# Moving a four-byte tile of GpSimd's from ahead of the SiLU halves to the end of the SBUF allocation

## The chip, the cores and the metric

The kernel runs on one core of a Trainium2 chip. The metric is the device time of one execution in microseconds (us). Three executions of the kernel before took 629.55, 629.67 and 630.14 us, so its median is 629.67 us. A fourth execution was recorded by the profiler; its own time and its span are in the table below.

## What is computed

The input x has 2048 rows of 640 values. The reference, cut to what matters:

```python
xn = layernorm(x)                       # over the 640 columns, no scale, no bias
q, k, v = split(xn @ wqkv)              # 32 heads of 20; wqkv is 640 x 1920
# row i attends to rows i, i-2, ... i-14 (8 rows, 2 apart); rows before 0 masked
s = attention(q, k, v) @ wo             # softmax over the 8; wo is 640 x 640
h = silu(xn @ w1) @ w2                  # w1 is 640 x 1536, w2 is 1536 x 640
out = x + s * silu(h)
```

All arrays are float32.

## The kernel before, in words

**Precision by halves.** TensorE multiplies in the type `float32r`. To keep float32 accuracy every operand of a large product is kept as a high half, rounded to that type, and a low half, the remainder. One product a*b is three matmuls: high by high, low by high, high by low. The halves of the normalized x are `TH` and `TL`, those of the attention's output are `OH` and `OL`, those of silu(xn @ w1) are `SH` and `SL` ("silu's halves"), and those of a weight lie one behind the other in one tile of the ring `w`, which has 7 slots.

**Groups.** The 2048 rows are worked in four groups of 512. A group has 4 row tiles of 128 (the index t). Each group goes through these stages on TensorE, in this order:

- `qkv_phase` (lines 950 to 952, and line 883 for the first quarter of the first group): xn @ wqkv in four quarters of the heads. `TH`/`TL` are stationary (loaded by LDWEIGHTS, 128 x 128), the weights stream past them (the moving operand).
- `ffn_phase`, which weaves `up` (lines 1114 to 1116: one 128-column block of w1 is stationary, `TH`/`TL` stream in rows of 512) with `down` (function `down`, matmuls at lines 990 and 992: `SH` or `SL` is stationary, a block of w2 streams). There are 12 blocks, so 12 `up` and 12 `down` in each group.
- `wo_phase` of the group before stands behind the first `up` (lines 990 and 992 again: `OH`/`OL` stationary, wo streams). For the last group `wo_last` does this at the very end, in another order: row tile by row tile, with the five weight tiles taken one after the other inside.

The products by w2 and by wo have 640 output columns, more than one PSUM bank holds. The helper `tm_mm` (lines 986 to 992) splits each into a matmul of 384 columns (line 990) and one of 256 columns (line 992) with the same stationary operand. The text calls two such matmuls a **pair**. `down` makes 12 pairs for a block: for each of the 4 row tiles `SH` by the high half and `SH` by the low half of w2 (8 pairs), and then for each row tile `SL` by the high half (4 pairs). `wo_phase` makes 3 pairs for each row tile and each of 5 weight tiles.

Between the matmuls the other engines work: ScalarE evacuates PSUM and makes the high halves (line 1127 writes `sh`, line 1128 writes the unrounded copy `sf`), VectorE makes the low halves (line 1129 writes `sl` from `sf` and `sh`) and does the whole attention (lines 768 to 808, tiles `kv`, `q`, `pr`, `l`, `o`). The order of the instructions on all engines comes from a planner (class `Weave`), which works from fixed costs and does not know addresses.

**The tile that moves.** `MARK` is one float32 per partition. At lines 910 to 912 GpSimd runs three subtractions of one column into it. Its value is never read. The instruction exists to make GpSimd wait for a tile of x to be normalized before it goes on.

**Where the tiles lie.** All SBUF tiles come from one pool with one buffer each (line 297, allocations at lines 318 to 349), and lie in a partition in the order of allocation. In the built program each starts at a multiple of 32 bytes. The last of the 7 weight tiles ends at byte 94976 of a partition, a multiple of 256. `epst` (4 bytes), `sd` (32 bytes) and `mark` (4 bytes) follow and take 32 bytes each, so `sh0` starts at 95072. Then come `sh1`, `sh2`, `sl0` to `sl2` (2048 bytes each), `mv`, `z`, `kv`, `q`, `o`, `pr`, `l`, `xin`, `gate`, `xr`, `sf` and `turn`. `th`, `tl` and `w` lie ahead and start at multiples of 256. `OH` and `OL` are views into the same memory as `TH` and `TL`, but 16 floats (64 bytes) further on for `OH` (the constant `OAT`), which is stationary in `wo_phase`.

The text names the place of a tile by what is left when its start is divided by 128: `w`, `TH` and `TL` 0, `OH` and `OL` 64, `sh` and `sl` 96, and `kv`, `q`, `o`, `pr`, `xin`, `gate`, `xr`, `sf`, `turn` 0.

Of the kernel before, what the change touches and what calls it, by code (L numbers as in the profile page):

```python
# [23 lines left out]
T = 4  # L24
# [269 lines left out]
def local_attention_silu_ffn(ctx: ExitStack, tc: tile.TileContext, x, wqkv, wo, w1, w2, out):  # L294
# [20 lines left out]
    def tiles(name, n, shape, dtype=F32):  # L315
        return [sb.tile(shape, dtype, name=f"{name}{i}") for i in range(n)]

    ident = sb.tile([P, P], F32, name="ident")
    def small(name, *shape):
        return sb.tile([P, *shape], F32, name=name)  # L320
# [10 lines left out]
    OH, OL = chunks(TH, OAT), chunks(TL, OAT)  # L331
    TH, TL = chunks(TH, 0), chunks(TL, 0)
    WR = tiles("w", RING, [P, 2 * D], F32R)
    epst, SD, MARK = small("epst", 1), small("sd", 2, T), small("mark", 1)
    SH = tiles("sh", NS, [P, TOK], F32R)
    SL = tiles("sl", NS, [P, TOK], F32R)
    MV = small("mv", T, 2)
# [9 lines left out]
    XR = tiles("xr", 3, [P, D])  # L347
    SF = sb.tile([P, TOK], F32, name="sf")
    TURN = sb.tile([P, TOK], F32, name="turn")
    ACC = [psum.tile([P, TOK], F32, name=f"acc{i}") for i in range(6)]  # L350
    ROT = [psum.tile([P, TOK], F32, name=f"rot{i}") for i in range(2)]
    carry = [dram.tile([2, NQ, 2, T, CQ], F32, name=f"carry{par}") for par in range(2)]
# [5 lines left out]
    def take(kind, n):  # L358
        i = count[kind] % n
        count[kind] += 1  # L360
        return i

    def bank():
        i = take("acc", 6)
        return ACC[i], ("acc", i)

# [20 lines left out]
    def pe(dur, fn, reads, writes, spans=()):  # L387
        add("PE", dur, fn, reads, writes, spans=spans)
        clock[0] += dur
# [262 lines left out]
    def both(k):  # L652
        return [k + (0,), k + (1,)]

    def piece(tile_of, k):
        return tile_of.rearrange("p t d -> p (t d)")[:, k * TOK:(k + 1) * TOK]
# [14 lines left out]
    def join(frm, into, kinto, reads, i, c, hi, lo, at=0.0, of=None):  # L671

        b, kb = frm
        kh, kl = t_keys(i, [c], kinds=["th"]), t_keys(i, [c], kinds=["tl"])
        act(2 * TOK, lambda: nc.scalar.activation(
            into.bitcast(U16).rearrange("p t (n h) -> p h t n", h=2),
            b.bitcast(U16).rearrange("p (h t n) -> p h t n", h=2, t=T), AF.Copy),
            both(kb) + reads, kinto, 150, more=0.3, at=at, spans=chunk_span(of, c, True) if of else ())
        act(TOK, lambda: nc.scalar.activation(hi.rearrange("p (t n) -> p t n", t=T), into, AF.Copy), kinto + reads, kh, 0)
        dve(TOK, lambda: nc.vector.tensor_tensor(  # L680
            out=lo.rearrange("p (t n) -> p t n", t=T), in0=into,
            in1=hi.bitcast(F32).rearrange("p (t n) -> p t n", t=T), op=OP.subtract),
            kinto + reads + kh, kl, 0, lock=True, late=SUB_LATE, spans=chunk_span(of, c) if of else ())

    def turn_x(c, i, at):
        keys = [("xin", t) for t in range(T)]
        by = (TURN, ("turn",)) if c % 2 == 0 else (piece(G, X_BY[c]), ("buf", X_BY[c]))
        to = piece(G, c), ("buf", c)
# [3 lines left out]
    def spare(s, q):  # L692

        return KV[q][:, s, HALO:, :].rearrange("p t m -> p (t m)")[:, :TOK], (("own", "val")[s], q, "x")
# [11 lines left out]
    def turn_o(g, c, i, out, into, at=0.0):  # L706
# [3 lines left out]
        xp = [(piece(XIN, k), ("xp", k)) for k in range(DC)]  # L710
        by, to = ((xp[0], xp[1]), (xp[2], xp[3]), (xp[4], (TURN, ("turn",))), (xp[1], xp[3]))[c]
        if g < NG - 1:
            by, to = (TURN, ("turn",)), (SF, ("sf",))
        if out:
# [118 lines left out]
    def first_quarter(i):  # L833
# [3 lines left out]
        def warm(n, where):  # L837
            for k in range(n):
                nc.tensor.transpose(where[:, tsl(k % T)], ident, ident)
# [64 lines left out]
        for n, step in enumerate(FIRST.split()):  # L904
            if n == len(PARTS):
                pe(0.11 * WARM2, lambda: warm(WARM2, ACC[5]), [], [("acc", 5)])
            (turn if len(step) == 2 else product)(*map(int, step))
# [10 lines left out]
    def qkv_phase(g, i, io):  # L918
        if g == TURNS:
            for c in O_FIRST:  # L920
                by, to = (((TURN, ("turn",)), spare(1, 0)), (spare(0, 1), spare(1, 1)))[c]
                join(to, by[0].rearrange("p (t n) -> p t n", t=T), both(by[1]), [], io, c, OH[io][:, c, :], OL[io][:, c, :])
# [232 lines left out]
    def ffn_phase(g, i, ix, io):  # L1155
# [10 lines left out]
        if g < TURNS:  # L1166
            lent = ((TURN, ("turn",)), spare(1, 0)), (spare(0, 1), spare(0, 0)), ((TURN, ("turn",)), spare(0, 0)), (spare(0, 1), spare(1, 1))
            for v in ((0, 0), (0, 1), (1, 0), (1, 1)):
# [75 lines left out]
```

## Time and profile before

| what | number |
|---|---|
| median of 3 executions | 629.67 us |
| profiled execution, its own time | 629.49 us |
| its span, first to last instruction | 627.7 us |
| TensorE (PE) busy | 621.7 us, 99% of the span |
| weight loads (PEld) busy | 563.1 us |
| VectorE (DVE) busy | 542.7 us |
| ScalarE (ACT) busy | 264.2 us |
| GpSimd (POOL) busy | 114.8 us |
| matmuls | 3415 |

PE is the matmul side of TensorE and PEld its weight loads, which run beside the matmuls. Matmuls are pipelined: the duration of one as the profile shows it is longer than the distance to the next one's start. So where a rate is wanted, the text takes the distance between starts. The difference between the profiled execution's own time and its span, 1.8 us, lies around the program's instructions.

### The profile page before, as it was taken

To read this page: it belongs to the slowest core of one execution; us is meant where nothing else is said; L and a number is where in the kernel's file an instruction comes from. 1 tells how busy PE (TensorE), PEld (TensorE's weight loads), DVE (VectorE), ACT (ScalarE), POOL (GpSimd) and SP (SyncE) were. 2 spreads that over 40 slices of the span, in tenths; PEclk is the share of its full clock that TensorE was granted. 3 is DMA by queue.
4 is the path that set the end of the run, shared out by engine and by line. 5 is a ranking of instruction groups with operands and counts; after the bars stand their busy time and mean duration, and the time that the engine had idled before them with its cause. 6 is when DMAs were issued, how large, how long until landed. Compare 5 with 4: busy or idle time off the path is not lost.

```text
span 627.7 us, 9038 instructions
## 1 busy us (share of the span) xinstructions
PE 621.7 (99%) x3415; PEld 563.1 (90%) x3415; DVE 542.7 (86%) x545; ACT 264.2 (42%) x490; POOL 114.8 (18%) x165
## 2 busy tenths in 40 slices
PE   8999999999999999999999999999999999999997
PEld 7888999998889999999888999999988999999897
DVE  6699899999788988999969999998745999998834
ACT  4445455463536216353434503445543343243220
POOL 5800000001110142111221114211222211111100
PEclk9999999999999999999999999999999999999999
DMA  9999999599999999775899999997599998678652
GB/s 312 292 319 317 317 394 373 187 325 268 257 331 299 310 264 294 236 205 147 203 307 252 317 368 256 331 233 215 141 239 271 294 344 238 202 218 243 192 185 85
DMA packets 99260, 166.07 MB, mean 265 GB/s; under 512 B 31008, under 2 KB 60672, under 8 KB 99216
## 3 DMA queue, kind: packets, MB, share of 16 engines
q1 hardware_dynamic: 72720, 85.77, 48.6%
q0 software_dynamic: 25952, 79.31, 44.1%
q8 instruction: 27, 0.44, 0.3%
q10 hardware_dynamic: 544, 0.41, 0.2%
q14 instruction: 17, 0.14, 0.1%
HBM read 107.91 MB, written 34.16 MB: 226 GB/s over the span
## 4 chain that ended last, share of the span: by engine, by line
PE 98%; DMA 0%; DVE 0%; issue 0%
PE acc L990 23%; PE acc L992 15%; PE acc L950 10%; PE acc L952 10%; PE acc L951 10%; PE rot L1114 9%; PE rot L1116 9%; PE rot L1115 9%; PE acc L883 2%; PE rot L630 1%; DMA xin<-in_A_x_dram 0%; PE rot L867 0%; PE rot L1100 0%; DVE st L852 0%; PE rot L826 0%; DVE gate L1068 0%
## 5 line engine op out<-in xcount | busy, mean ns | idle before, releaser
L990 PE MATMUL acc<-w,sh 128*128 128x384 f32 x384 | 115.2, 338 | 0.0
L950 PE MATMUL acc<-w,th 128*128 128x512 f32 (+2 forms) x300 | 113.2, 377 | 0.0
L952 PE MATMUL acc<-w,th 128*128 128x512 f32 (+2 forms) x300 | 112.8, 376 | 0.0
L951 PE MATMUL acc<-w,tl 128*128 128x512 f32 (+2 forms) x300 | 112.8, 376 | 0.0
L992 PE MATMUL acc<-w,sh 128*128 128x256 f32 x384 | 107.5, 280 | 0.0
L768 DVE TENSOR_TENSOR pr<-q,kv 128x2560 f32<-128x2560 f32 x32 | 90.2, 2819 | 13.3 <-DMA kv<-kv 13.1
L1127 ACT ACTIVATE sh<-rot 128x512 fp32r<-128x512 f32 x48 | 28.7, 599 | 166.0 <-PE rot L1116 165.9
L1114 PE MATMUL rot<-th,w 128*128 128x512 f32 x240 | 94.4, 393 | 0.0
L1116 PE MATMUL rot<-th,w 128*128 128x512 f32 x240 | 93.6, 390 | 0.0
L1115 PE MATMUL rot<-tl,w 128*128 128x512 f32 x240 | 93.5, 390 | 0.0
L800 DVE TENSOR_TENSOR pr<-q,kv 128x2560 f32<-128x2560 f32 x32 | 90.3, 2822 | 0.7
L771 DVE TENSOR_REDUCE l<-pr 128x128 f32<-128x2560 f32 x32 | 90.0, 2814 | 0.3
L558 POOL DMA_DIRECT2D w<-half_q x52 | 37.4, 719 | 236.6 <-DVE pr L805 97.7
L558 POOL DMA_DIRECT2D w<-half_w x72 | 38.6, 536 | 215.1 <-PE acc L992 99.8
L805 DVE TENSOR_TENSOR pr<-pr 128x1280 f32<-128x1280 f32 x64 | 75.5, 1180 | 1.4
L992 PEld LDWEIGHTS acc<-w,sh 128*128 128x128 f32 x384 | 72.5, 189 | 1.1
L990 PEld LDWEIGHTS acc<-w,sh 128*128 128x128 f32 x384 | 72.1, 188 | 1.0
L952 PEld LDWEIGHTS acc<-w,th 128*128 128x128 f32 x300 | 56.3, 188 | 8.8
L951 PEld LDWEIGHTS acc<-w,tl 128*128 128x128 f32 x300 | 56.3, 188 | 8.6
L950 PEld LDWEIGHTS acc<-w,th 128*128 128x128 f32 x300 | 56.3, 188 | 8.5
L990 PE MATMUL acc<-w,sl 128*128 128x384 f32 x192 | 59.0, 338 | 0.0
L727 ACT ACTIVATE kv<-acc 128x320 f32<-128x320 f32 x64 | 28.1, 441 | 69.2 <-PE acc L952 67.9
(115 smaller groups left out, 1040.8 us busy)
## 6 DMA issues: line engine op xcount, KB each, us to landing
w<-half_w POOLq DMA_DIRECT2D x72, 640.0 KB, 5.3
w<-half_q POOLq DMA_DIRECT2D x39, 512.0 KB, 4.9
half_w<-w SPq DMA_DIRECT2D x24, 640.0 KB
kv<-kv SPq DMA_DIRECT2D x16, 560.0 KB
kv<-kv SPq DMA_DIRECT2D x16, 420.0 KB
w<-half_wo POOLq DMA_DIRECT2D x10, 640.0 KB, 5.6
gate<-in_B_w_dram SPq DMA_DIRECT2D x16, 320.0 KB
w<-half_q POOLq DMA_DIRECT2D x13, 384.0 KB, 7.9
```

The lines of the kernel that those rows point to most:

```text
L558: add("POOL", 1.0, lambda: nc.gpsimd.dma_start(both, src), [("half", u), ("half", u, "more")], [kh, kl], due + 10, nbytes=2 * n * P * 4)
L768: dve(2560, lambda t=t: nc.vector.tensor_tensor(out=PR, in0=win(qq[:, t:t + 2, :], W, 0), in1=win(kv[:, 0, t:t + 2, :], W, CQ), op=OP.mult ...
L771: dve(2560, lambda t=t: nc.vector.tensor_reduce(out=l[:, t:t + 2].rearrange("p t w h -> p (t w h)"), in_=PR.rearrange("p t w (h d) -> p (t ...
L800: dve(2560, lambda t=t, v=v: nc.vector.tensor_tensor(out=PR.rearrange("p t w (h d) -> p t (w h) d", d=DH), in0=e[:, t:t + 2].rearrange("p ...
L950: nc.tensor.matmul(o, hi, wh, start=c == 0, stop=False)
L951: nc.tensor.matmul(o, lo, wh, start=False, stop=False)
L952: nc.tensor.matmul(o, hi, wl, start=False, stop=c == DC - 1)
L990: nc.tensor.matmul(a[t][0][:, :CA], st, w[:, :CA], start=first, stop=last)
L992: nc.tensor.matmul(b[t // 2][0][:, h * CB:(h + 1) * CB], st, w[:, CA:], start=first and h == 0, stop=last, skip_group_check=True)
L1114: nc.tensor.matmul(h, wh[:, cs], TH[i][:, c, :], start=c == 0, stop=False)
L1115: nc.tensor.matmul(h, wh[:, cs], TL[i][:, c, :], start=False, stop=False)
L1116: nc.tensor.matmul(h, wl[:, cs], TH[i][:, c, :], start=False, stop=c == DC - 1)
```

## The change

`MARK` is taken out of the line that allocates it between `sd` and `sh0`, and allocated behind `turn`, the last tile of the pool. No instruction, wait, size or order is edited. What follows from the 32-byte starts: `sh0` begins at 95040 instead of 95072, and every tile from `sh0` to `turn` begins 32 bytes lower, so that `sh` and `sl` go from place 96 to place 64, and `kv`, `q`, `o`, `pr`, `xin`, `gate`, `xr`, `sf` and `turn` from place 0 to place 96. `ident`, `th`, `tl`, `w`, `epst` and `sd` stay.

```diff
     WR = tiles("w", RING, [P, 2 * D], F32R)
-    epst, SD, MARK = small("epst", 1), small("sd", 2, T), small("mark", 1)
+    epst, SD = small("epst", 1), small("sd", 2, T)
     SH = tiles("sh", NS, [P, TOK], F32R)
     SL = tiles("sl", NS, [P, TOK], F32R)
     MV = small("mv", T, 2)
...
     SF = sb.tile([P, TOK], F32, name="sf")
     TURN = sb.tile([P, TOK], F32, name="turn")
+    MARK = small("mark", 1)
     ACC = [psum.tile([P, TOK], F32, name=f"acc{i}") for i in range(6)]
```

## The prediction

> **What bounds the kernel now.** I read the page first, for the engines' shares and the chain that ended last.
>
> ```profile
> span 627.7 us, 9038 instructions
> ...
> PE 621.7 (99%) x3415; PEld 563.1 (90%) x3415; DVE 542.7 (86%) x545; ACT 264.2 (42%) x490; POOL 114.8 (18%) x165
> ...
> PE 98%; DMA 0%; DVE 0%; issue 0%
> PE acc L990 23%; PE acc L992 15%; PE acc L950 10%; PE acc L952 10%; PE acc L951 10%; PE rot L1114 9%; PE rot L1116 9%; PE rot L1115 9%; PE acc L883 2%; PE rot L630 1%; DMA xin<-in_A_x_dram 0%; PE rot L867 0%; PE rot L1100 0%; DVE st L852 0%; PE rot L826 0%; DVE gate L1068 0%
> ```
>
> The matmuls fill the span, and 98% of the chain is matmul behind matmul. Lines 990 and 992, which share the pair matmuls of `down` and of the wo stages, hold 38% of it. Next, the view of waits for PE:
>
> ```profile
> PE rot L839 <- POOL ident masks.py:199: 1.4, 1, 1.4
> PE rot L867 <- DVE xin L857: 0.7, 1, 0.7
> ```
>
> These two waits, both in the first microseconds, are all that it lists. So the time is a count of matmuls times the distance from one start to the next, and an edit that adds or removes no instruction can act only through that distance, or by making another engine so late that PE waits. The groups that keep forms apart give the count of the matmuls whose stationary operand moves:
>
> ```profile
> L990 PE MATMUL acc<-w,sh 128*128 128x384 f32 x384 | 115.2, 338 | 0.0
> L992 PE MATMUL acc<-w,sh 128*128 128x256 f32 x384 | 107.5, 280 | 0.0
> ...
> L990 PE MATMUL acc<-w,sl 128*128 128x384 f32 x192 | 59.0, 338 | 0.0
> L992 PE MATMUL acc<-w,sl 128*128 128x256 f32 x192 | 53.8, 280 | 0.0
> ```
>
> That is 384 + 192 = 576 pairs. Then I asked whether a pair costs the same everywhere, in the timeline of PE. One block of `down` (start in us, modelled duration):
>
> ```profile
> 88.87 0.34 PE L990 MATMUL acc<-w,sh 128*128 128x384 f32 x1
> 89.04 0.28 PE L992 MATMUL acc<-w,sh 128*128 128x256 f32 x1
> ...
> 92.39 0.38 PE L630 MATMUL rot<-ident,xin 128*128 128x128 f32 x2
> ```
>
> Between the first and the last row lie 12 pairs (8 by `sh`, 4 by `sl`): 3.52 / 12 = **293.3 ns a pair**. A stretch of `wo_phase`:
>
> ```profile
> 203.53 0.33 PE L990 MATMUL acc<-w,th 128*128 128x384 f32 x1
> 203.70 0.28 PE L992 MATMUL acc<-w,th 128*128 128x256 f32 x1
> ...
> 206.97 0.33 PE L990 MATMUL acc<-w,th 128*128 128x384 f32 x1
> ```
>
> Again 12 pairs of 384 and 256 columns, by the same weight ring: 3.44 / 12 = **286.7 ns**. And `wo_last`:
>
> ```profile
> 608.23 0.34 PE L990 MATMUL acc<-w,th 128*128 128x384 f32 x1
> 608.41 0.28 PE L992 MATMUL acc<-w,th 128*128 128x256 f32 x1
> ...
> 611.83 0.34 PE L990 MATMUL acc<-w,th 128*128 128x384 f32 x1
> ```
>
> 12 pairs: 3.60 / 12 = **300.0 ns**. The reader is to see that the same two instructions run at three paces, with no wait in any of the three stretches. In `down` the stationary operand stands at place 96, in both wo stages at place 64 (`OH`, `OL`), and the streamed weights at place 0 in all three.
>
> **The change part by part.** It adds, removes and reorders no instruction, DMA or wait, so nothing is queued behind anything new. Three things can cost or gain.
>
> *GpSimd's own instruction.*
>
> ```profile
> L910 POOL TENSOR_TENSOR mark<-xin 128x1 f32<-128x1 f32 x3 | 0.6, 195 | 4.0 <-issue 1.8 <-DVE xin L857 1.5 <-POOL w L571 0.7
> ```
>
> Three of 195 ns, which write one column per partition somewhere else. No one reads it: 0.
>
> *The 576 pairs of `down`.* Their stationary operand goes from 96 to 64, which is the very place, against the same ring, that `wo_phase` has. If the place makes the difference, a pair goes from 293.3 to 286.7 ns: 576 x 6.6 = 3.8 us. The bounds are the other rows: no change at all, 0, and the pace of `wo_last`, 576 x (300.0 - 293.3) = 3.9 us more. I take the row nearest to it in form. `down` and `wo_phase` both run the row tiles inside, keep one weight tile for all of them, and use a stationary operand for two or four pairs' matmuls in a row; `wo_last` takes another weight tile and another stationary operand with every pair. From the 3.8 us I take off 0.2: the first pairs behind a change of stage do not yet run at the settled pace (26 such stretches by the order of `up` and `down`, at up to 7 ns). So **-3.6 us**. The Trainium skill speaks against it: "SBUF — State Buffer", in the table under "A bandwidth-pool intuition that's wrong (but worth ruling out)", gives TensorE a second, independent read port for LDWEIGHTS, so where the weights to be loaded lie should not touch the stream, and by that the sum would be 0. The same page, under "Specifications (TRN2)", speaks of 16-byte cachelines, to which both places are equally well aligned: again 0. The three paces above show that something slows a pair by up to 13 ns; they do not show that it is the place.
>
> *Everything else that moves 32 bytes.* VectorE's and ScalarE's operands go from place 0 to 96. Before, there are instructions that already work at 96, beside the like of them at 0:
>
> ```profile
> L1129 DVE TENSOR_TENSOR sl<-sf,sh x48: 679/685/5333, 68.6 to 600.1; 128x512 fp32r<-128x512 f32 x48
> ```
>
> ```profile
> L680 DVE TENSOR_TENSOR tl<-xin,th 128x512 fp32r<-128x512 f32 x16 | 10.9, 684 | 7.4 <-ACT th L679 7.4
> L1127 ACT ACTIVATE sh<-rot 128x512 fp32r<-128x512 f32 x48 | 28.7, 599 | 166.0 <-PE rot L1116 165.9
> L1128 ACT ACTIVATE sf<-rot 128x512 f32<-128x512 f32 x48 | 28.4, 593 | 4.5 <-DVE sl L1129 4.5
> L634 ACT ACTIVATE th<-rot 128x512 fp32r<-128x512 f32 x13 | 7.6, 598 | 15.3 <-PE rot L630 15.3
> ```
>
> Line 1129 reads and writes at 96 in 685 ns (the median), line 680 reads and writes only at 0 in 684; ScalarE writes `sh` at 96 in 599 and `th` at 0 in 598. So I cost these at 0. DMAs into `xin`, `kv`, `xr` and `gate` at 96 do not occur before; no row prices them. The transposes, too, have their stationary operand moved:
>
> ```profile
> L630 PE MATMUL rot<-ident,o 128*128 128x128 f32 x40 | 5.7, 272 | 0.0
> ```
>
> There are 80 in all (40 here, 12 at line 630 by `xin`, 20 at 867, 8 at 826); at the 6.6 ns that the place may be worth to a whole pair they move the time by 0.5 us at most either way, and I take 0.
>
> *What is late next if PE gains.* The tightest place that I found is in the last group, where PE transposes the last rows of the attention's output:
>
> ```profile
> 594.45 0.49 DVE L808 TENSOR_TENSOR o<-pr 128x320 f32<-128x320 f32 x1
> ```
>
> ```profile
> 596.25 0.44 PE L826 MATMUL rot<-ident,o 128*128 128x128 f32 x2
> ```
>
> VectorE is done at 594.94, PE comes at 596.25: 1.31 us to spare. VectorE's run-up to this begins at 477.43, with the first scores of the group, behind a wait that hangs on PE's own progress (the k and v just made, carried over by a DMA):
>
> ```profile
> 477.43 2.83 DVE L768 TENSOR_TENSOR pr<-q,kv 128x2560 f32<-128x2560 f32 x1 [8.11 <-DMA kv<-kv]
> ```
>
> So the gain of the first three groups (432 pairs) moves both, and only that of some 120 pairs in the last group eats into the reserve: 120 x 6.6 = 0.8 us of 1.31. It holds, without much over.
>
> The sum: 629.49 (the profiled execution's own time, 1.8 us of it around the span of 627.7) - 3.6 = 625.9 us. The median of the runs lies 0.2 above the profiled one, so I say **626.0 us**, 0.6% under 629.67.
>
> **Rivals.**
>
> *A, the forecast:* `down` takes the pace of `wo_phase`. For it: form and place are then alike. Against it: `wo_last` has that place as well, and is the slowest. With 0.5 us for the transposes and the same again for pairs that do not settle at once: 625.2 to 627.2 us.
>
> *B, the place does not matter.* The paces then come from the order of the operands: `wo_phase` goes high, high, low through each row tile, `down` takes all high ones first and then all low ones. For it: inside `down` the pace is the same by `sh` and by `sl` (338 and 280 ns in both groups above), so the pace goes with the stage, and each stage has only one place. 629.5 us, between 629.0 and 630.2. That the edit might not move the tiles at all comes to the same time; the sizes and the 32-byte starts leave it little chance.
>
> *C, the slower side: place 64 is the one at which load and stream disturb each other in lockstep.* The stationary operand's reads and the stream's then meet at a fixed distance of half of 128 bytes, and it depends on the order of the matmuls whether they miss each other (286.7) or collide each time (300.0). In `down` they collide, and a pair takes 300.0 ns: 576 x 6.7 = 3.9 us more, 633.4 us. It decides against the forecast as soon as the mean pair of `down` is above 293.3. For it: `wo_last`, with operands at the same places. Against it: `down` has the order of `wo_phase` in all but the low halves.
>
> *D, the other moved tiles cost something.* VectorE's 86% of work, or the k and v transfers, run slower at 96, by an amount that the 685 against 684 ns does not let me expect. From 477.4 to 594.9 VectorE has 117.5 us; a slowdown of 1.1% uses up the 1.31 us, and at 3% the end comes 3.5 - 1.3 = 2.2 us later: 631.7 us without A, about 629 with it.
>
> **How the numbers follow.** Chances: A 0.60, B 0.16, C 0.15, D 0.09. The predicted time is A's, 626.0 us. The range must leave out no more than 2 in 10: from A's lower end, 625.2, over B up to D's 631.7; I leave out C and a little at the edges. A measurement of this kernel can tell about 0.2%, 1.26 us, from no change: faster means under 628.4, slower over 630.9. A is faster, B the same, C and most of D slower: 0.60, 0.16 and 0.24.
>
> **What would show it right or wrong.** Right: in the timeline of the changed kernel 12 pairs of `down` take 3.44 us instead of 3.52; the groups of line 990 by `sh` and `sl` fall from 338 ns towards 332; `wo_phase`, `wo_last` and the `up` matmuls keep their distances; VectorE's groups keep their means; PE's waits stay the two at the start; the span is near 624.1. B is seen in an unchanged 3.52, C in 3.60, D in a new wait of PE at line 826 or in longer means at lines 768 to 808. What would make the prediction wrong is above all that place 64 is not what makes `wo_phase` quick: I have two stages at that place, and they disagree by 13 ns.

## The result and the profile after

| | before | after |
|---|---|---|
| median | 629.64 us (4 runs) | 626.59 us (4 runs, 626.20 to 626.76) |
| ratio, with its 95% interval | | 0.9949 [0.9932, 0.9966] |
| span of the profiled execution | 627.7 us | 625.0 us |

The change made the kernel 3.05 us faster. The page of the changed kernel:

```profile
span 625.0 us, 9038 instructions
...
PE 619.4 (99%) x3415; PEld 559.8 (90%) x3415; DVE 542.8 (87%) x545; ACT 264.3 (42%) x490; POOL 114.8 (18%) x165
...
PE 98%; DMA 1%; DVE 0%; issue 0%
```

The same instructions, the same DVE and ACT, and PE is still the whole chain. Its waits (engine, line, who was waited for, us in total, times, longest) are still the two at the start. One line was added above them, so line 839 is now 840 and 990 is 991:

```profile
PE rot L840 <- POOL ident masks.py:199: 1.4, 1, 1.4
PE rot L868 <- DVE xin L858: 0.4, 1, 0.4
```

The groups whose stationary operand moved:

```profile
L991 PE MATMUL acc<-w,sh 128*128 128x384 f32 x384 | 113.2, 334 | 0.0
L993 PE MATMUL acc<-w,sh 128*128 128x256 f32 x384 | 107.1, 279 | 0.0
...
L991 PE MATMUL acc<-w,sl 128*128 128x384 f32 x192 | 57.8, 332 | 0.0
L993 PE MATMUL acc<-w,sl 128*128 128x256 f32 x192 | 53.6, 279 | 0.0
```

Before, these were 338 and 280 ns. Their distances show it better. One block of `down` in the timeline of PE, first row to last 12 pairs:

```profile
229.17 0.33 PE L991 MATMUL acc<-w,sh 128*128 128x384 f32 x1
229.34 0.28 PE L993 MATMUL acc<-w,sh 128*128 128x256 f32 x1
...
232.61 0.40 PE L1115 MATMUL rot<-th,w 128*128 128x512 f32 x1
```

3.44 / 12 = 286.7 ns, exactly the pace of `wo_phase`, where it was 293.3. But `wo_last`, none of whose operands moved, changed as well. Two rows of the same timeline, 12 pairs apart:

```profile
606.09 0.33 PE L991 MATMUL acc<-w,th 128*128 128x384 f32 x1
...
609.53 0.33 PE L991 MATMUL acc<-w,th 128*128 128x384 f32 x1
```

3.44 / 12 = 286.7 ns too; before it was 300.0. And the `up` matmuls, not moved either, became slower at their beginning. A run of 30 of them, from its first row to the first pair behind it, before:

```profile
232.90 0.40 PE L1114 MATMUL rot<-th,w 128*128 128x512 f32 x1
...
239.71 0.34 PE L990 MATMUL acc<-w,sh 128*128 128x384 f32 x1
```

and after:

```profile
232.61 0.40 PE L1115 MATMUL rot<-th,w 128*128 128x512 f32 x1
...
239.45 0.34 PE L991 MATMUL acc<-w,sh 128*128 128x384 f32 x1
```

6.81 us against 6.84; in the trace's nanoseconds 6810 against 6846. Before, the distances begin 235, 227, 226, 227; after, they begin 235, 234, 235, 225, 230, 236, 229, 232, 231 and only then stay at 226 to 227. This occurs in the 17 runs of `up` that follow a `down`, each 36 ns longer. The kernel before had such long runs too, behind `wo_phase`, the stage that ran at 286.7 ns there:

```profile
219.01 0.40 PE L1114 MATMUL rot<-th,w 128*128 128x512 f32 x1
...
225.86 0.34 PE L990 MATMUL acc<-w,sh 128*128 128x384 f32 x1
```

6.85 us for 30 matmuls (6848 ns), and 6849 ns behind the other two passes of `wo_phase`. So a run of `up` starts slower behind pairs at 286.7 ns than behind pairs at 293.3, and after the change `down` is such a stage as well.

One difference lies in the very first microseconds, in the twenty transposes of the identity that keep TensorE busy before data arrive:

```profile
L840 PE MATMUL rot<-ident 128*128 128x128 f32 x20 | 4.5, 424 | 1.4 <-POOL ident masks.py:199 1.4
```

Before it was 374 ns on average, and in e1 and e2 of the experiments below 400 and 417: the first ones come 213 ns apart and later ones 109, and how many come slowly differs from trace to trace (13 of the 19 distances before, all of them after, in e4 and in e5). No tile of theirs moved, so I do not count it as the change's, but no second profile of one kernel shows how much of it is chance.

Summed over all matmuls, from each start to the next, the two traces differ by: `down` -3.36 us, `wo_last` -0.65, `up` +0.62, all of `qkv` +0.21, all transposes +0.48 (0.34 of it the twenty at the start with the wait behind them). The sum is -2.70, the difference of the spans (627.7 and 625.0).

### The profile page after: what moved, and what is told of

The parts are those of the page before. It is cut to its first block, busy times and chain, and to the rows that moved or that the text cites. A ratio compares the mean times of both kernels' runs of the same rounds, so it can differ in the third digit from the quotient of the medians.

```text
span 625.0 us, 9038 instructions
## 1 busy us (share of the span) xinstructions
PE 619.4 (99%) x3415; PEld 559.8 (90%) x3415; DVE 542.8 (87%) x545; ACT 264.3 (42%) x490; POOL 114.8 (18%) x165
## 4 chain that ended last, share of the span: by engine, by line
PE 98%; DMA 1%; DVE 0%; issue 0%
PE acc L991 22%; PE acc L993 15%; PE acc L953 10%; PE acc L951 10%; PE acc L952 10%; PE rot L1117 9%; PE rot L1116 9%; PE rot L1115 9%; PE acc L884 2%; PE rot L631 1%; DMA xin<-in_A_x_dram 1%; PE rot L868 0%; PE rot L1101 0%; DVE st L853 0%; PE rot L827 0%; DVE gate L1069 0%
## 5 line engine op out<-in xcount | busy, mean ns | idle before, releaser
L991 PE MATMUL acc<-w,sh 128*128 128x384 f32 x384 | 113.2, 334 | 0.0
L769 DVE TENSOR_TENSOR pr<-q,kv 128x2560 f32<-128x2560 f32 x32 | 90.2, 2819 | 12.6 <-DMA kv<-kv 8.8
L801 DVE TENSOR_TENSOR pr<-q,kv 128x2560 f32<-128x2560 f32 x32 | 90.3, 2822 | 0.7
```

What stands on the lines that cost most here:

```text
L769: dve(2560, lambda t=t: nc.vector.tensor_tensor(out=PR, in0=win(qq[:, t:t + 2, :], W, 0), in1=win(kv[:, 0, t:t + 2, :], W, CQ), op=OP.mult ...
L801: dve(2560, lambda t=t, v=v: nc.vector.tensor_tensor(out=PR.rearrange("p t w (h d) -> p t (w h) d", d=DH), in0=e[:, t:t + 2].rearrange("p ...
L991: nc.tensor.matmul(a[t][0][:, :CA], st, w[:, :CA], start=first, stop=last)
```

## The experiments

The first theory: the place of the stationary operand of `down` sets the pace of its pairs. Its rivals: the other tiles that moved (kv, q, pr, xin and so on); the order of a stage's matmuls rather than any place (B). `small` in the diffs allocates a tile, and a tile of 4 to 32 bytes takes 32.

**e1: only silu's halves move.**

```diff
-    epst, SD, MARK = small("epst", 1), small("sd", 2, T), small("mark", 1)
+    epst, SD = small("epst", 1), small("sd", 2, T)
     SH = tiles("sh", NS, [P, TOK], F32R)
     SL = tiles("sl", NS, [P, TOK], F32R)
+    MARK = small("mark", 1)
```

> MARK is allocated right behind silu's halves: sh and sl go from place 96 to 64 as in the changed kernel, every tile behind them (mv, kv, q, o, pr, xin, gate, xr, sf, turn) stays where it was before. Theory 1 (the place of the stationary operand sets the pace of a pair): the whole gain, 626.6 us within 0.5, 12 pairs of down in 3.44 us. Rival (the other moved tiles brought it, or a part of it): 629.6 us, or something between. Side question: wo_last ran at 300 ns a pair before and at 287 after, though none of its operands moved; if it inherits the pace from the stage ahead of it, it runs at 287 here.

Measured 626.45 us, ratio 0.9949 [0.9934, 0.9964]: the whole gain. 12 pairs of `down` took 3.45 us, `wo_last` ran at 286.7 ns.

**e2: only the rest moves.**

```diff
     SL = tiles("sl", NS, [P, TOK], F32R)
+    PAD = small("pad", 24)
```

> The kernel before with 96 idle bytes behind silu's halves: sh and sl stay at place 96, all tiles behind them go from place 0 to place 96, as in the changed kernel. Theory 1: no gain, 629.6 us within 0.5, 12 pairs of down in 3.52 us, wo_last at 300 ns. Rival (the rest brings the gain): about 626.6. My rival D of the prediction (VectorE or the transfers are slower at 96): over 630, with longer means at lines 768 to 808.

Measured 629.90 us, 1.0003 [0.9993, 1.0012]: nothing. From first row to last 12 pairs:

```profile
230.20 0.34 PE L991 MATMUL acc<-w,sh 128*128 128x384 f32 x1
...
233.73 0.40 PE L1115 MATMUL rot<-th,w 128*128 128x512 f32 x1
```

3.53 us, and `wo_last` at 300. The trace has one wait of PE that the kernel before does not have, 0.4 us at line 1115 for ScalarE's `sf`, 68 us into the span; the changed kernel, with `sf` at the same place, has none there. VectorE at place 96 is as quick as at 0, in the changed kernel's groups and here:

```profile
L801 DVE TENSOR_TENSOR pr<-q,kv 128x2560 f32<-128x2560 f32 x32 | 90.3, 2823 | 0.7
L769 DVE TENSOR_TENSOR pr<-q,kv 128x2560 f32<-128x2560 f32 x32 | 90.2, 2819 | 13.0 <-DMA kv<-kv 9.0 <-DMA kv<-carry 3.8
L772 DVE TENSOR_REDUCE l<-pr 128x128 f32<-128x2560 f32 x32 | 90.1, 2815 | 0.3
```

The page of before has 2822, 2819 and 2814. So rival D of the prediction falls, and e1 and e2 together show that the gain is that of `sh` and `sl`.

**e3: `sh` at 64, `sl` at 96.**

```diff
     SH = tiles("sh", NS, [P, TOK], F32R)
+    MARK = small("mark", 1)
     SL = tiles("sl", NS, [P, TOK], F32R)
```

(MARK is taken out of its old line here as well.)

> MARK lies between sh and sl: sh at place 64, sl at 96, the rest as before. Theory 1, pair by pair: the 384 pairs by sh take 286.7 ns and the 192 by sl 293.3, so two thirds of the gain, 627.5 us within 0.5. Rival (the pace belongs to the stage as a whole, as a state in which the matmuls have settled): sh and sl keep one common pace, 286.7 or 293.3, and the time is 626.6 or 629.6.

Measured 628.60 us, 0.9982 [0.9973, 0.9991]. Neither expectation holds: not the 627.5 of the theory, and no common pace. Two blocks of `down` in a row, each 8 pairs by `sh` and then 4 by `sl`:

```profile
253.67 0.34 PE L991 MATMUL acc<-w,sh 128*128 128x384 f32 x1
...
255.98 0.34 PE L991 MATMUL acc<-w,sl 128*128 128x384 f32 x1
...
257.15 0.34 PE L991 MATMUL acc<-w,sh 128*128 128x384 f32 x1
...
259.52 0.34 PE L991 MATMUL acc<-w,sl 128*128 128x384 f32 x1
```

The first 8 pairs follow an `up` and take 2.31 us, 289 ns a pair; the second 8 follow pairs by `sl` at 96, and take 2.37, 296 ns. (Before and after the change, the two blocks of such a run differ by less than 2 ns a pair.) Pair by pair (384 + 256 columns, ns) a first block goes 177+117, 175+118, 174+113, 170+116 and stays at 286.7; a second one goes 180+122, 179+118, 177+119, 177+114, 175+118, 177+119, 181+119, 181+117, and settles nowhere. The operands stand at the same places in both. So I had to widen the theory: **the place decides at which paces a stage can settle, and the state that the stage before leaves decides at which of them it does.** At place 64 there are two, 286.7 and 300, as `wo_last` shows before and after: in e1 and in the changed kernel it went from one to the other though nothing that its matmuls read or write had moved. What this state is, no run shows; e8 below shows best that it is handed on.

**e4 and e12: place 0.** In e4 `epst`, `SD`, `MARK` and `MV` all lie ahead of `SH`, which makes it an odd multiple of 128 bytes; in e12 all four lie behind `SL`, which makes it a multiple of 256. Everything further back stays.

e4, with `epst`, `SD` and `MARK` on lines of their own:

```diff
-    epst, SD, MARK = small("epst", 1), small("sd", 2, T), small("mark", 1)
+    epst = small("epst", 1)
+    SD = small("sd", 2, T)
+    MARK = small("mark", 1)
+    MV = small("mv", T, 2)
     SH = tiles("sh", NS, [P, TOK], F32R)
     SL = tiles("sl", NS, [P, TOK], F32R)
-    MV = small("mv", T, 2)
```

> epst, sd, MARK and mv all lie ahead of sh, so sh and sl stand at place 0, like w; all tiles behind them stay as before. Theory 1a (only that the stationary block starts at a multiple of 64 bytes counts): as at 64, 286.7 ns a pair, 626.6 us. Theory 1b (its distance from the stream within 128 bytes counts, and half of 128 is the good one): not 286.7 but 293 to 300 ns, 629.5 to 633.5 us.

> silu's halves at place 0 once more, but at a multiple of 256 bytes (all four small tiles behind them), where e4_place0 had an odd multiple of 128. If only the distance within 64 or 128 bytes counts, all stages repeat e4_place0: down settles at 286.7 ns with 168 + 118, wo_last at 300, 628.3 us. If 256 counts, down settles at another pace or in another way.

e4: 628.29 us, 0.9977 [0.9967, 0.9987]. e12: 629.48 us, 0.9998 [0.9988, 1.0008]. Twelve pairs of `down` in e4:

```profile
242.86 0.33 PE L992 MATMUL acc<-w,sh 128*128 128x384 f32 x1
...
246.30 0.40 PE L1116 MATMUL rot<-th,w 128*128 128x512 f32 x1
```

and in e12:

```profile
243.07 0.34 PE L992 MATMUL acc<-w,sh 128*128 128x384 f32 x1
...
246.59 0.39 PE L1116 MATMUL rot<-th,w 128*128 128x512 f32 x1
```

3.44 and 3.52 us: 286.7 and, on average, 293.3 ns. In e4 the pace is that of theory 1a, and 1b is refuted; the time is neither's. e4 settles at the same pace as the changed kernel, but gives more back: the first pairs of a run take 184+120, 179+117 (before: 175+117, 172+117), the `up` runs grow by 59 ns instead of 36, and `wo_last` enters at 300. e12 did not repeat e4, against what I expected if 64 or 128 bytes were the whole rule. It does not settle at one pace at all: its pairs go round between 291 and 297 ns (292, 296, 292, 293, 292, 297, 291, 294, ...). Either 256 bytes count, or another state is entered. The runs do not tell these apart.

**e5: place 32.** Only `epst` ahead of `SH`, the other three small tiles behind `SL`.

> Only epst lies ahead of sh, so sh and sl stand at place 32; mv and all tiles behind stay as before. So far the settled pair of down took 293.3 ns at place 96, 286.7 at 64 and 286.7 at 0. Theory 1b (the distance within 128 bytes counts, 32 and 96 are mirror images): 293.3 ns a pair, about 629.6 us. Theory 1a (a start at a multiple of 64 bytes is quick, any other slow): the same 293.3. Against both, if odd places differ among themselves: another number, and then the place within 64 bytes is not the rule.

630.11 us, 1.0009 [0.9995, 1.0023]. Twelve pairs:

```profile
243.28 0.34 PE L992 MATMUL acc<-w,sh 128*128 128x384 f32 x1
...
246.80 0.39 PE L1116 MATMUL rot<-th,w 128*128 128x512 f32 x1
```

3.52 us, 293.3 ns, as at 96. Both theories had said so; the run does not choose between them.

**e6: the same done to `wo_phase`.** In the changed kernel:

```diff
-    OH, OL = chunks(TH, OAT), chunks(TL, OAT)
+    OH, OL = chunks(TH, 8), chunks(TL, 8)
```

> The changed kernel with OH and OL 8 floats instead of 16 behind TH and TL: the stationary operand of wo_phase and wo_last goes from place 64 to 32, nothing else moves. Theory 1 (place of the stationary operand): wo_phase leaves 286.7 ns a pair, to what e5_place32 shows for place 32; at 293.3 its 180 pairs cost 1.2 us more. The rival of the prediction (B: wo_phase is quick by its order of high, high, low): it stays at 286.7 ns, 626.6 us.

628.02 us, 0.9982 [0.9967, 0.9997]. The stretch of `wo_phase`, 12 pairs from first row to last:

```profile
203.90 0.34 PE L991 MATMUL acc<-w,th 128*128 128x384 f32 x1
...
207.42 0.34 PE L991 MATMUL acc<-w,th 128*128 128x384 f32 x1
```

3.52 us: `wo_phase` went from 286.7 to 293.3 ns with its order untouched, and `wo_last` as well (in the trace 293.5 on average). This is rival B's end: the order alone did not make it quick. The time is 1.4 us over the changed kernel's, near the 1.2 expected, though one of the four executions took 630.04.

**e7: the ring moves instead.** The changed kernel with 32 idle bytes ahead of `w`:

```diff
+    PAD = small("pad", 8)
     WR = tiles("w", RING, [P, 2 * D], F32R)
```

> The changed kernel with 32 idle bytes ahead of the weight ring: w goes from place 0 to 32, sh and sl to 96, and everything behind them to where it was before; the distance between the stationary operand and the stream in down is still 64, but the stationary block again starts at an odd multiple of 32. Theory 1b (distance): down settles at 286.7 ns. Theory 1a (the stationary block's own start): 293.3 ns, as before. In qkv, up and the wo stages the distance changes by 32; if the distance counts there as well, their matmuls of 512 and 384 columns and the pairs of wo_phase change their pace, and the whole may be slower than 630.

640.83 us, 1.0179 [1.0164, 1.0193]. Twelve pairs of `down`, and the first `up` group:

```profile
246.84 0.34 PE L992 MATMUL acc<-w,sh 128*128 128x384 f32 x1
...
250.44 0.40 PE L1116 MATMUL rot<-th,w 128*128 128x512 f32 x1
```

```profile
L1116 PE MATMUL rot<-th,w 128*128 128x512 f32 x240 | 95.7, 399 | 0.0
```

`down` settles at 3.60 / 12 = 300 ns, in 24 of its 26 runs; the last two settle at 286.7, with operands at the same places. So neither expectation holds: by theory 1b all runs should have been at 286.7, by 1a at 293.3. The halves stand at 96, as before, and yet no run is at 293.3: it is not the stationary block's own start alone that counts but where it stands against the stream, 64 apart, and at 64 the second of the two paces was mostly entered. `wo_phase`, now 32 apart, went to 293.4 ns. The matmuls of 512 columns, which are 0 apart in the changed kernel and 32 apart here, went from 227 to 233 ns from start to start.

**e8: 64 apart in every stage.** Ring at place 64, `OAT` 32, `QAT` 32, `th` and `tl` resized so that they still start at multiples of 128.

> The changed kernel with 64 idle bytes ahead of the weight ring and the offsets of OH, OL and the first quarters set so that stationary and streamed operand are 64 apart in every stage; in the changed kernel they are 0 apart in up and in all later quarters of qkv (1260 matmuls of 384 or 512 columns). Theory 1b: down and wo_phase stay at 286.7 ns, and up and qkv settle at another pace than their 226.7 ns for 512 columns; at 3 ns less it is 3.8 us off, 622.8 us, at 3 ns more 630.4. Theory 1a: no stage changes its settled pace, 626.6 us within 0.7 for the settling behind each change of stage.

635.08 us, 1.0088 [1.0074, 1.0102]. Matmuls of 512 columns in `qkv` took 233 ns, `up` 232 on average, `wo_phase` 293.9 on average. Neither expectation holds here either. `down` settles at 286.7 ns in 18 of its 26 runs and at 300 in the other 8, all with the same places. In the second group (and so in the last) the two take turns. Here are the first rows of its stages `down`, `up`, `down`, `up`, `down`, `up`; a `down` has 24 pairs, an `up` 30 matmuls:

```profile
227.95 0.34 PE L992 MATMUL acc<-w,sh 128*128 128x384 f32 x1
...
235.14 0.40 PE L1116 MATMUL rot<-th,w 128*128 128x512 f32 x1
...
242.14 0.34 PE L992 MATMUL acc<-w,sh 128*128 128x384 f32 x1
...
249.03 0.39 PE L1116 MATMUL rot<-th,w 128*128 128x512 f32 x1
...
255.91 0.34 PE L992 MATMUL acc<-w,sh 128*128 128x384 f32 x1
...
263.10 0.40 PE L1116 MATMUL rot<-th,w 128*128 128x512 f32 x1
```

`down` takes 7.19, 6.89 and 7.19 us (300, 287 and 300 ns a pair), `up` between them 7.00 and 6.88 (233 and 229 ns a matmul). No tile moves during an execution, so one place allows more than one pace, and which of them a stage takes goes with the stage before it: the widened theory in one trace. And 64 apart is not good as such: for 512 columns 0 apart, as in the kernel before, is better by 6 ns in `qkv`. In one of the two buffers `OL` stands 128 bytes away from `OH` within 256, and `TL` from `TH`, which they did not before; so `wo_last`, two of the three passes of `wo_phase`, and `qkv` and `up` of the first and third groups are not a clean comparison. The second pass of `wo_phase` uses the other buffer and settles at 293.3 ns: 64 apart does not exclude that pace.

**e9 and e10: the first quarters.** The changed kernel with `QAT = 32` and `QAT = 56` instead of 48, to look for a still faster version.

> The changed kernel with the weights of the first group's quarters (480 columns) at place 0 instead of 64 inside their ring slots: 240 matmuls, which take 219.5 ns on average and settle near 216, get the distance 0 at which those of 512 settle at 32 cycles' worth (226.7 - 512 x 0.4167 = 13.3 ns) over the plain stream. If the distance rules here too, they settle at 480 x 0.4167 + 13.3 = 213.3 ns and the kernel gains 0.6 us on the changed one, 626.0; the rival (a row of 480 settles by its own length, whatever the distance) says 626.6.

> As e9_first_place0, but at place 96. In e7_w_place32 the first quarters had this distance and their 240 matmuls took 52.1 us in place of 52.7; the same here gives 626.0 us. By the rule found for pairs (an odd multiple of 32 is the slow middle) they should not gain: 626.6 us or more. These two cannot both hold.

e9: 627.22 us, 0.9959 [0.9945, 0.9974]; e10: 627.10 us, 0.9953 [0.9939, 0.9968]. No gain on the changed kernel (0.9949), though one of e10's four executions took 625.46. e9's 626.0 did not come, and its time is over the rival's too; e10 is as the rule for pairs had it. The 240 matmuls of 480 columns took 52.9 us in e9, 53.6 in e10, 52.8 in the changed kernel. In e7, with the distance of e10, they took 52.1: the distance alone does not fix their pace either.

**e11: the kernel before with one more transpose ahead of `wo_last`.**

```diff
+        pe(0.11, lambda: nc.tensor.transpose(lastb[:, :P], ident, ident), ["consts"], [klast])
         for t in range(T - 1):
```

> The kernel before, every tile at its old place, with one more 128 x 128 transpose of the identity on TensorE right ahead of wo_last, into the free PSUM bank. Theory 2 (at a distance that is a multiple of 64 a stage settles at 286.7 or at 300 ns, and the state in which it is entered picks which): wo_last can change from 300 to 286.7, its 45 pairs then take 0.6 us less, and added work makes the kernel 0.4 us faster, 629.2. Rival (wo_last's pace belongs to its operands or to the idle engines beside it): 300 ns as before and 629.8 us. If the transpose happens to lead into the same state, nothing changes, and the run does not decide.

629.60 us, 1.0001 [0.9992, 1.0010], `wo_last` at 300 as before. By its own terms it does not decide: the transpose may have led into the same state. That the pace of `wo_last` does not belong to its operands, as the rival has it, e1 had already shown.

## Why the prediction was right

The time (626.59 us) lies 0.6 from the forecast (626.0) and the mechanism of A is the one that the runs show. By its steps:

- **What bounds the kernel** and that only distances between matmuls could act: right. PE's waits are the same two, and the sum of the distances by stage gives the difference of the spans.
- **The 576 pairs**, forecast -3.6 us: measured -3.36. The settled pace came out as forecast to the nanosecond (3.44 us for 12 pairs). The 0.2 us taken off for unsettled pairs was too little (3.8 - 3.36 = 0.44 was missing): the first two pairs of each of the 26 runs take 294 and 293 ns after against 292 and 288 before, so they lose instead of gaining.
- **The rest at nothing**: right, e2 has 1.0003 [0.9993, 1.0012]; so D falls. GpSimd's instruction as well.
- **"`wo_phase`, `wo_last` and the `up` matmuls keep their distances"**: wrong for two of three. `wo_last` gained 0.65 us and `up` lost 0.62. I had not seen that a stage hands its state on to the next. The loss in `up` could have been read from the profile before, where the runs behind `wo_phase` took 6848 and 6849 ns and those behind `down` 6810: 17 x 0.038 = 0.6 us. That the two cancel is luck; the total was nearer than its terms deserve.
- **B** is refuted by e6. The prediction had for it that each stage has only one place, so the profile before could not tell the two apart; moving `OH` could. **C** did not come about here, but its pace is real: at 64 apart the same matmuls settle at 300 ns in `wo_last` before, in 24 of 26 runs of `down` in e7 and in 8 of 26 in e8. That load and stream collide there, as C had it, no run shows. Had `down` entered there, the kernel would have been slower, and nothing in the profile before told which of the two it would be. That it entered at 286.7 is luck as well; the 0.15 for C was no wasted caution.
- **The Trainium skill**, "SBUF — State Buffer" ("A bandwidth-pool intuition that's wrong (but worth ruling out)"): it gives TensorE a second, independent read port for LDWEIGHTS. The prediction drew from it that the place should not matter; e1 and e6 disagree with that, with 6.7 ns a pair either way. Its 16-byte cachelines ("Specifications (TRN2)") do not separate the places either: 96 and 64 are both multiples of 16.

## What to carry to other kernels

Where TensorE is the whole chain, compare the start-to-start distance of equal matmuls between stages. If it differs, look at where stationary and streamed operand lie against each other: here 32 bytes in the allocation order were worth 6.7 ns in 293 on 576 pairs. Any new small tile, however unimportant, shifts everything allocated behind it; put it last, or where nothing that TensorE loads lies behind it. And time the result: a place that makes one stage quick can leave the next one slower, and the same place can give two paces.

## What the runs showed of the hardware that was not expected

- A pair of 384 and 256 columns settled at one of three paces, 286.7, 293.3 and 300.0 ns. Where stationary and streamed operand were an odd multiple of 32 bytes apart through a whole stage it was 293.3 (`down` before and in e2, e5 and e11, `wo_phase` and `wo_last` in e6 and e7). At multiples of 64 all three occurred, 293.3 in the second pass of `wo_phase` in e8 alone, and some stages settled at no one pace (e12, the second blocks of e3).
- At 64 apart the pace goes with the state in which the stage is entered: `wo_last` ran at 300 ns in the kernel before, e2, e4, e5, e11 and e12 and at 286.7 after, in e1, e3, e9 and e10, with its operands at the same places. In e3 two equal blocks took 289 and 296 ns a pair, one behind an `up`, one behind pairs at 96. In e8 `down` took 287 and 300 ns a pair by turns.
- After a change of stage the pace takes up to ten matmuls to settle, before and after the change in the same way each time for the same pair of stages (6810 or 6846 ns for a run of 30 behind a `down`); in e8 such runs took 6883 to 6996.
- Why it is so inside the memory or the array, and whether 256 bytes count (e4 against e12), stays open.
